# Expert slots: turning the tokens with VectorE and ScalarE instead of TensorE

## The chip, the cores and the metric

One core of one Trainium2 chip. The metric is the device time of one execution in microseconds, the median of three runs. The engines are TensorE (matmuls, PE in the profile; its weight loads are PEld), VectorE (DVE), ScalarE (ACT), GpSimd (POOL) and SyncE (SP, which issues most transfers).

## The reference: what is computed

Three stages over 4608 tokens of 512 values, all in float32:

```python
kv  = einsum('bhsd,bhse->bhde', k, v)           # attention without softmax, 8 batches, 8 heads
x   = rmsnorm(einsum('bhsd,bhde->bhse', q, kv)) * g_norm    # 4608 x 512
h   = x @ w_in                                  # 512 -> 2048
x   = gate(h) @ w_out                           # gate: h above 1, 0 below -1, (h+1)**2/4 between
e   = argmax(normalised x @ normalised expert_emb.T / tau)  # one of 8 experts per token
out = softmax_weight * (relu(x @ w1[e]) @ w2[e])            # 512 -> 1024 -> 512
```

## The kernel before, in words

The attention and the dense block come first (up to about 945 us). Each tile of 128 tokens that leaves the dense block is routed: its rows, 512 values and 16 of bookkeeping (`ROW` is 528), are scattered to the region of their expert in `xs`. Then come the expert **slots**. A slot is one tile of up to 128 tokens that share an expert; there are at most 43 (`NSLOT`), and 41 are run before a branch that asks whether more are wanted. The first four (`FULL`) belong to an expert that is known early, and have code of their own; slots 4 and on read a table, made by VectorE, of which rows, which expert and which half of the weight ring they use.

What a slot does:

- `x_load` (L750) brings the tile `xr[t]` from `xs`, tokens on partitions. `loads_ahead` issues it four slots ahead (`X_AHEAD`); seven buffers (`xr`, `row`) hold tiles.
- The tile is turned, so that the 512 values lie on partitions, in four blocks of 128. Before the change TensorE does it: `tr_x` (L768) issues four transposes by an identity (L771) into a PSUM bank `xp`, right after layer 1 of the slot before; `split_x` (L774) then has ScalarE copy the bank as fp32r, `x[:, 0]` (L778), and VectorE subtract that copy from the bank (helper `sub`, L192), so that `x[:, 1]` holds what the rounding left over.
- Layer 1, `l1` (L842): 24 matmuls of 128x128 by 512 columns. Four blocks by two halves of the 1024 hidden values, each as three products (`PASSES`: high by high, high by low, low by high).
- For slots 4 and on, `turn_h` (L888) turns the 1024 hidden values: VectorE transposes squares of 32x32, 16 instructions of 32 partitions by 256 elements from PSUM (L897). Host code laid out `w1` so that the squares land where layer 2 wants them. `split_h` (L904) makes the two halves of `hT` with ReLU: ScalarE's copy (L912), VectorE's subtraction (L914), twice.
- Layer 2, `l2` (L920): 24 matmuls. `finish` (L927) weighs the rows (ScalarE's `ex`, L932, and `ys`, L938; two small VectorE operations) and GpSimd scatters them to `out` (L941).

TensorE's order is written by `slots`: layer 1 of slot t, the transposes for slot t+1, layer 2 of slot t-1. So the work of VectorE and ScalarE on a slot has most of a slot's time to finish.

The order on the other engines comes from a planner, `Flow`: each piece of work is a generator that yields the engine and an estimated cost ahead of every instruction, `ev` for events and `get` for buffers. The piece that could start first goes next on its engine; among those within 0.05 us, the lower priority number. `turn_h` and `split_h` have 0, `finish` 0.5. Every engine then runs its instructions in the order that the planner wrote.

Weights lie in two rings of two halves, `ra` (layer 1) and `rb` (layer 2). `load_next` (L786) is called once per slot and ring, but moves data only in the first slot of an expert (`cond`), for the expert after it: two transfers of 2 MB each (L807), once the half to be filled is no longer read by TensorE and the loads before it on the same ring have landed.

Of the kernel before, what the change touches and what calls it, by code (L numbers as in the profile page):

```python
# [7 lines left out]
F32 = mybir.dt.float32  # L8
F32R = mybir.dt.float32r
# [3 lines left out]
AF = mybir.ActivationFunctionType  # L13
# [5 lines left out]
P = 128  # L19
# [3 lines left out]
DM = 512  # L23
# [6 lines left out]
ROW = 528  # L30
# [123 lines left out]
def tile_kernel(ctx: ExitStack, tc: tile.TileContext, qT, k, v, g2, w_in, w_out, emb, tau, w1, w2, cst, tri, out):  # L154
    nc = tc.nc
# [6 lines left out]
    NSLOT = TOK // P + NE - 1  # L162
# [4 lines left out]
    FULL = (NBLK - 1) * TB // NE // P  # L167
# [7 lines left out]
    keep = ctx.enter_context(tc.tile_pool(name="keep", bufs=1))  # L175
# [6 lines left out]
    f = Flow()  # L182

    def bank(name, tag, shape=(P, DM), bufs=1):
        return ps.tile(list(shape), F32, name=name, tag=tag, bufs=bufs)
# [5 lines left out]
    def sub(eng, out_, a, hi):  # L191
        eng.tensor_tensor(out=out_, in0=a, in1=hi.bitcast(F32), op=ALU.subtract)  # L192
# [10 lines left out]
    for name, n in {  # L203
        "h": 2, "cl": 2, "g": 2, "xT": 2, "sp": 2, "raw0": 1, "raw1": 1, "raw2": 1, "raw3": 1, "t0": 1, "t1": 1, "t2": 1, "t3": 1, **{f"kv{i}": 1 for i in range(7)}, "qt": 1, "xk": 1, "op": 1, "xp": 1, "kvp": 1,
        "kvd0": 1, "kvd1": 1, "acc0": 1, "acc1": 1, "acc2": 1, "row": NTB, "r": 1, "xr": 4, "hb00": 1, "hb01": 1, "hb10": 1, "hb11": 1,
        "y0": 1, "y1": 1, "xT2": 2, "ht": 2, "hT": 2, "small": 1, "dots": 1,
    }.items():
        f.put(name, n)


    kvd2 = keep.tile([P, 2 * 4 * P], F32, name="kvd2")
    nc.gpsimd.memset(kvd2, 0.0)
    kvd = [kvd2[:, i * 4 * P : (i + 1) * 4 * P].rearrange("p (a c) -> p a c", a=4) for i in range(2)]
    consts_ = {}
# [268 lines left out]
    dots = {}  # L483
# [61 lines left out]
    pools = {}  # L545
# [183 lines left out]
    xr = {}  # L729
    xT2 = {}  # L730
    ht = {}
    hT = {}
# [3 lines left out]
    def reg(eng, ap, hi, lo=0):  # L736
        return eng.value_load(ap, min_val=lo, max_val=hi)
# [30 lines left out]
    def tr_x(t):  # L768
        xp = bank("xp2", "xp", (P, 4, P))
        for c in range(4):  # L770
            nc.tensor.transpose(out=xp[:, c], in_=xr[t][:, c * P : c * P + P], identity=consts_["cs"][:, 0:P])  # L771
        return xp

    def split_x(t, xp):  # L774
        yield "get", "xT2"
        yield "act", 0.48
        x = xT2[t] = pools["x"].tile([P, 2, 4, P], F32R, name="xT2", tag="xT2", bufs=2)
        nc.scalar.activation(out=x[:, 0], in_=xp, func=AF.Copy)  # L778
        yield "dve", 0.6
        sub(nc.vector, x[:, 1], xp, x[:, 0])  # L780
        f.put("xp")
        f.set(("x2", t))

    loads = {"a": [None, None], "b": [None, None]}

    def load_next(t, which):  # L786
# [30 lines left out]
    def product(out, lhsT, t, which, c0, start, stop):  # L817
        ring = ra if which == "a" else rb
        if t < FULL:
            nc.tensor.matmul(out=out, lhsT=lhsT, rhs=ring[:, 0, c0 : c0 + 512], start=start, stop=stop)  # L820
            return
        m = nc.tensor.matmul(  # L822
            out=out, lhsT=lhsT, rhs=ring[:, bass.ds(pars[t], 1), c0 : c0 + 512].rearrange("p a f -> p (a f)"),
            start=start, stop=stop,
        )
        cur, prev = loads[which]
        for d in cur:
            tc.declare_no_dep(_ins(m), _ins(d), reason="the load fills the other half of the ring")
        if prev is not None:
            for q, d in enumerate(prev):  # L830
                if q == c0 // (8192 // NPC):
                    need(m, d, "an earlier load filled this half of the ring")
                else:
                    tc.declare_no_dep(_ins(m), _ins(d), reason="the load fills other columns")
# [3 lines left out]
    def hb(t, hf):  # L838

        return f"hb{0 if t < FULL else t % 2}{hf}"  # L840

    def l1(t):  # L842
        x = xT2[t]
        for hf in range(2):
            yield "get", hb(t, hf)
            for dk in range(4):
                yield "pe", 0.71
                if dk == hf == 0 and t >= FULL:
                    pars[t] = reg(nc.tensor, ord_["sch"][t : t + 1, 3:4], 1)
                if dk == 0:  # L850
                    h = bank("h2", HB[hb(t, hf)], bufs=2 if HB[hb(t, hf)] == "h" else 1)
                for n, (xa, wa) in enumerate(PASSES):
                    product(
                        h, x[:, xa, dk], t, "a", dk * 2048 + wa * 1024 + hf * 512, dk == 0 and n == 0,
                        dk == 3 and n == 2,
                    )
            f.add(relu(t, hf, h) if t < FULL else turn_h(t, hf, h), 0)

    def relu(t, hf, h):
        if hf == 0:  # L860
            yield "get", "ht"
            ht[t] = pools["h"].tile([P, 8, P], F32, name="hr", tag="ht", bufs=2)
        yield "act", 0.6
        nc.scalar.activation(
            out=ht[t].rearrange("p c (q a) -> p q c a", q=4)[:, 2 * hf : 2 * hf + 2],
            in_=h.rearrange("p (q c a) -> p q c a", q=2, c=8), func=AF.Relu,
        )
        f.put(hb(t, hf))
        f.set(("hs", t, hf))
# [18 lines left out]
    def turn_h(t, hf, h):  # L888

        if hf == 0:  # L890
            yield "get", "ht"
            ht[t] = pools["h"].tile([P, 8, P], F32, name="ht", tag="ht", bufs=2)
        for i in range(4):
            for q in range(2):
                yield "dve", 0.36
                r, s = slice(32 * i, 32 * i + 32), slice(64 * hf + 32 * q, 64 * hf + 32 * q + 32)
                nc.vector.transpose(  # L897
                    out=ht[t][s, :, r], in_=h[r, 256 * q : 256 * q + 256].rearrange("p (c a) -> p c a", c=8)
                )
        f.put(f"hb{t % 2}{hf}")  # L900
        if hf == 1:
            f.add(split_h(t), 0)
# [17 lines left out]
    def l2(t, fcs):  # L920
        if fcs[0] == 0:
            yps[t] = bank("y", f"acc{t % 2}")
        for fc in fcs:
            for n, (ga, wa) in enumerate(PASSES):
                product(yps[t], hT[t][:, ga, fc], t, "b", fc * 1024 + wa * 512, fc == 0 and n == 0, fc == 7 and n == 2)
# [240 lines left out]
    def loads_ahead(t):  # L1166
        if FULL <= t < NSLOT:
            yield "ev", "table"
            yield "get", "xr"
            yield "sp", 2.9 if t == FULL else 1.9 if t < FULL + NE - 1 else 0.9  # L1170
            x_load(t)

    def slots(start, end):

        for t in range(start, end + 1):
            if t < end:
                f.add(loads_ahead(t + X_AHEAD), 0)
                f.set(("slot", t))
                yield "ev", ("x2", t)
                if t == 0:  # L1180
                    for q in range(4):
                        yield "ev", ("ring", "a", q)
                yield from l1(t)
                if FULL <= t + 1 < NSLOT:
                    yield "ev", "table"
                    load_next(t + 1, "a")
                f.put("xT2")
                if t + 1 < NSLOT:
                    yield "ev", ("xr", t + 1)
                    yield "get", "xp"  # L1190
                    yield "pe", 0.43
                    f.add(split_x(t + 1, tr_x(t + 1)), 0)
            if t > start:
                yield "get", f"y{(t - 1) % 2}"
                if t == 1:
                    for q in range(4):
                        yield "ev", ("ring", "b", q)
            for n in range(2):
                if t > start:
                    yield "ev", ("hT", t - 1, n)  # L1200
                    yield "pe", 2.81
                    l2(t - 1, range(4 * n, 4 * n + 4))
                if t < min(end, FULL):
                    if n == 0:
                        yield "get", "hT"
                        for hf in range(2):
                            yield "ev", ("hs", t, hf)
                    yield "get", f"hb1{n}"
                    yield "pe", 0.43
                    f.add(split_hp(t, n, tr_h(t, n)), 0)  # L1210
                    if n == 1:
                        f.put("ht")
            if t > start:
                f.put("hT")
                f.add(finish(t - 1), 0.5)
            if FULL <= t < end:
                load_next(t, "b")

    f.add(make_table(), 1)
    f.add(slots(0, SURE), 5)  # L1220
    f.add(second_expert(), 2)
    f.run()
    used = nc.values_load(ord_["sch"][0:1, 5:6], min_val=1, max_val=NSLOT)  # L1223
    with tc.If(used > SURE):
        f.add(slots(SURE, NSLOT), 5)
        f.run()
# [47 lines left out]
```

## Time and profile before

| what | value |
|---|---|
| median of three runs | 1448.8 us (1446.64 to 1449.76) |
| the profiled execution's own time | 1447.99 us |
| its span, first to last instruction | 1446.2 us |
| busy share of TensorE, VectorE, ScalarE, GpSimd | 96%, 77%, 43%, 26% |
| expert slots, first layer 1 to the last instruction | from about 945 us to the end |

The profile is of one execution. Busy time of TensorE is modelled, since its matmuls overlap; when it waited is read better from the list of waits, and how fast it ran from the starts in the timeline. A line of the timeline merges instructions of one kind: start, time to the end of the last, engine, line, operation, tiles, count; behind it in brackets the idle time before it and what ended that. "128x512 f32" is partitions by elements.

### The profile page before, as it was taken

How to read it: one execution, taken by the hardware profiler on the slowest of the kernel's cores; microseconds unless marked ns; L12 is line 12 of the kernel's file. 1: busy time of each engine (PE TensorE's matmuls, PEld its weight loads, DVE VectorE, ACT ScalarE, POOL GpSimd, SP SyncE). 2: the span in 40 equal slices, each digit the busy share in tenths (PEclk: the TensorE clock that was granted, in tenths of full speed). 3: DMA queues.
4: the chain of work that ended last, by engine and by line, in shares of the span. 5: the costliest groups of instructions: out<-in, count | busy, mean ns of one | idle time of the engine just before them, and what ended most of it. 6: DMA issues, size and time to landing. Idle time of an engine off the chain costs nothing. (4 is left out here: it accounts for less than half of the span.)

```text
span 1446.2 us, 24714 instructions
## 1 busy us (share of the span) xinstructions
PE 1391.8 (96%) x7474; PEld 1194.2 (83%) x7474; DVE 1120.5 (77%) x2629; ACT 618.5 (43%) x1259; POOL 377.0 (26%) x347
## 2 busy tenths in 40 slices
PE   6889999999999999999999999999999999999995
PEld 5768889889889888888889999878888888888884
DVE  5888989696969797978778756485887778888883
ACT  4766455545555554555555534332222222222221
POOL 1675233323233332333332332310000010000000
PEclk9999999999999999999999999999999999999998
DMA  9764654555655564545454200583111137774175
GB/s 290 240 223 169 204 193 166 190 196 183 216 191 177 176 232 170 180 167 180 164 181 162 69 31 1 222 334 112 53 46 45 46 136 278 273 288 178 46 298 207
DMA packets 85456, 249.99 MB, mean 173 GB/s; under 512 B 10190, under 2 KB 10446, under 8 KB 80592
## 3 DMA queue, kind: packets, MB, share of 16 engines
q1 hardware_dynamic: 79168, 229.21, 44.9%
q0 software_dynamic: 6160, 19.18, 3.4%
q8 instruction: 68, 1.11, 0.3%
q14 instruction: 60, 0.49, 0.1%
HBM read 423.87 MB, written 90.02 MB: 355 GB/s over the span
## 5 line engine op out<-in xcount | busy, mean ns | idle before, releaser
L1048 PE MATMUL acc<-rb,g 128*128 128x512 f32 x1728 | 448.5, 400 | 9.9 <-POOL rb L192 6.4
L1025 PE MATMUL h<-xT,ra 128*128 128x384 f32 x2304 | 441.3, 338 | 0.6 <-DVE xT L387 0.4
L1025 PEld LDWEIGHTS h<-xT,ra 128*128 128x128 f32 x2304 | 403.3, 188 | 17.6 <-DVE xT L387 0.6
L1048 PEld LDWEIGHTS acc<-rb,g 128*128 128x128 f32 x1728 | 319.8, 189 | 72.1 <-POOL rb L192 8.8
L897 DVE STREAM_TRANSPOSE ht<-h 32x256 f32<-32x256 f32 x592 | 264.1, 446 | 55.1 <-PE h L822 44.2
L192 POOL TENSOR_TENSOR sp<-sp 128x512 fp32r<-128x512 f32 x128 | 182.3, 1429 | 441.3 <-ACT sp L466 421.8
L561 DVE CUSTOM_DVE_ANT_0 tr<-row,en 128x512 bf16<-128x512 f32 x288 | 228.0, 796 | 3.0 <-ACT row L526 0.3
L822 PE MATMUL y<-rb,hT 128*128 x888 | 217.9, 401 | 5.1 <-DMA rb<-ws 5.1
L822 PE MATMUL h<-ra,xT 128*128 x888 | 213.9, 396 | 0.0
L822 PEld LDWEIGHTS y<-rb,hT 128*128 128x128 f32 x888 | 165.2, 189 | 43.3 <-issue 6.0
L822 PEld LDWEIGHTS h<-ra,xT 128*128 128x128 f32 x888 | 167.1, 188 | 40.4
L964 ACT ACTIVATE h<-h,neg 128x384 f32<-128x384 f32 x176 | 97.6, 554 | 214.8 <-DVE cl L957 214.8
L975 DVE TENSOR_TENSOR cl<-h,cl 128x384 f32<-128x384 f32 x176 | 97.4, 554 | 65.7 <-ACT cl L968 65.5
L980 ACT ACTIVATE g<-cl 128x384 fp32r<-128x384 f32 x192 | 100.7, 525 | 110.2 <-DVE cl L975 70.6
L957 DVE TENSOR_SCALAR cl<-h 128x384 f32<-128x384 f32 x192 | 105.8, 551 | 45.9 <-PE h L1025 44.9
L192 DVE TENSOR_TENSOR g<-cl,g 128x384 fp32r<-128x384 f32 x144 | 100.6, 698 | 31.9 <-ACT g L980 30.4
L968 ACT ACTIVATE cl<-cl,half 128x384 f32<-128x384 f32 x192 | 116.6, 607 | 0.0
L912 ACT ACTIVATE hT<-ht 128x512 fp32r<-128x512 f32 x74 | 46.2, 624 | 160.4 <-DVE ht L897 160.4
L941 POOL DMA_INDIRECT out<-ys,xr x24 | 23.4, 974 | 269.0 <-ACT ys L938 241.7
L778 ACT ACTIVATE xT<-xp 128x512 fp32r<-128x512 f32 x42 | 25.1, 598 | 159.3 <-PE xp L771 159.2
L466 ACT ACTIVATE sp<-sp 128x512 fp32r<-128x512 f32 x128 | 79.2, 622 | 12.6 <-DMA sp<-in_w 11.2
L192 POOL TENSOR_TENSOR g<-cl,g 128x384 fp32r<-128x384 f32 x48 | 53.4, 1113 | 88.8 <-ACT g L980 85.9
(156 smaller groups left out, 1079.2 us busy)
## 6 DMA issues: line engine op xcount, KB each, us to landing
ra<-ws SPq DMA_DIRECT2D x78, 2048.0 KB
rb<-ws SPq DMA_DIRECT2D x76, 2048.0 KB
ws<-sp SPq DMA_DIRECT2D x128, 512.0 KB
sp<-in_w SPq DMA_DIRECT2D x128, 256.0 KB
qt<-in_qT SPq DMA_DIRECT2D x33, 256.0 KB
raw<-in_w_in SPq DMA_DIRECT2D x16, 512.0 KB
raw<-in_w_out SPq DMA_DIRECT2D x16, 512.0 KB
kt<-in_k SPq DMA_DIRECT2D x26, 256.0 KB
```

The costliest lines, as they stand in the source:

```text
L192: eng.tensor_tensor(out=out_, in0=a, in1=hi.bitcast(F32), op=ALU.subtract)
L466: nc.scalar.activation(out=sp[:, 0], in_=r, func=AF.Copy)
L561: nc.vector.tensor_tensor_reduce(out=trash("tr", e % 2), in0=rows[blk, t][:, 0:DM], in1=en[:, e], scale=1.0, scalar=0.0, op0=ALU.mult, op1 ...
L822: m = nc.tensor.matmul(out=out, lhsT=lhsT, rhs=ring[:, bass.ds(pars[t], 1), c0 : c0 + 512].rearrange("p a f -> p (a f)"), start=start, sto ...
L897: nc.vector.transpose(out=ht[t][s, :, r], in_=h[r, 256 * q : 256 * q + 256].rearrange("p (c a) -> p c a", c=8))
L957: nc.vector.tensor_scalar(out=cl, in0=h, scalar1=-1.0, scalar2=1.0, op0=ALU.max, op1=ALU.min)
L964: nc.scalar.activation(out=over, in_=h, func=AF.Relu, bias=consts_["neg1"])
L968: nc.scalar.activation(out=cl, in_=cl, func=AF.Square, bias=consts_["half"], scale=0.5)
L975: nc.vector.tensor_tensor(out=cl, in0=over, in1=cl, op=ALU.add)
L980: nc.scalar.activation(out=g[:, 0], in_=cl, func=AF.Copy)
L1025: nc.tensor.matmul(out=h, lhsT=ra[:, wa, o : o + P], rhs=xT[blk][:, xa, dk], start=dk == 0 and n == 0, stop=dk == 3 and n == 2,)
L1048: nc.tensor.matmul(out=accs[t], lhsT=g[:, ga, t * P : t * P + P], rhs=rb[:, wa, df * 512 : df * 512 + 512], start=(df == 0 and n == 0), st ...
```

## The change

For slots 4 and on, TensorE's four transposes and their PSUM bank go. A new piece of work, `turn_x`, starts as layer 1 of the slot before starts. VectorE transposes the 128x512 tile in squares of 32x32, one instruction, into `xt`. This leaves each square turned, but in the quadrant of 32 partitions in which it was read. ScalarE then copies 32 partitions by 4x32 elements sixteen times, from quadrant i of `xt` to quadrant q of `xf`. From `xf`, in SBUF, the two halves of `xT2` are made as before: ScalarE's copy as fp32r, VectorE's subtraction. `xt` lies behind the padding rows in `kvd2`, which grows by 16 columns for it; `xt` and `xf` have one buffer each. Tiles 0 to 3 still go through TensorE.

```diff
--- before.py
+++ after.py
@@ -203,12 +203,12 @@
     for name, n in {
         "h": 2, "cl": 2, "g": 2, "xT": 2, "sp": 2, "raw0": 1, "raw1": 1, "raw2": 1, "raw3": 1, "t0": 1, "t1": 1, "t2": 1, "t3": 1, **{f"kv{i}": 1 for i in range(7)}, "qt": 1, "xk": 1, "op": 1, "xp": 1, "kvp": 1,
         "kvd0": 1, "kvd1": 1, "acc0": 1, "acc1": 1, "acc2": 1, "row": NTB, "r": 1, "xr": 4, "hb00": 1, "hb01": 1, "hb10": 1, "hb11": 1,
-        "y0": 1, "y1": 1, "xT2": 2, "ht": 2, "hT": 2, "small": 1, "dots": 1,
+        "y0": 1, "y1": 1, "xT2": 2, "ht": 2, "xt": 1, "xf": 1, "hT": 2, "small": 1, "dots": 1,
     }.items():
         f.put(name, n)
 
 
-    kvd2 = keep.tile([P, 2 * 4 * P], F32, name="kvd2")
+    kvd2 = keep.tile([P, 2 * 4 * P + ROW - DM], F32, name="kvd2")
     nc.gpsimd.memset(kvd2, 0.0)
     kvd = [kvd2[:, i * 4 * P : (i + 1) * 4 * P].rearrange("p (a c) -> p a c", a=4) for i in range(2)]
     consts_ = {}
@@ -781,6 +781,31 @@
         f.put("xp")
         f.set(("x2", t))
 
+    def turn_x(t):
+
+        yield "ev", ("xr", t)
+        yield "get", "xt"
+        yield "dve", 0.65
+        xt = kvd2[:, ROW : ROW + DM]
+        nc.vector.transpose(out=xt, in_=xr[t][:, 0:DM])
+        xt = xt.rearrange("p (c q b) -> p c q b", c=4, q=4)
+        yield "get", "xf"
+        xf = pools["h"].tile([P, 4, P], F32, name="xf")
+        for i in range(4):
+            for q in range(4):
+                yield "act", 0.29
+                r = slice(32 * i, 32 * i + 32)
+                nc.scalar.activation(out=xf[32 * q : 32 * q + 32, :, r], in_=xt[r, :, q], func=AF.Copy)
+        f.put("xt")
+        yield "get", "xT2"
+        yield "act", 0.6
+        x = xT2[t] = pools["x"].tile([P, 2, 4, P], F32R, name="xT2", tag="xT2", bufs=2)
+        nc.scalar.activation(out=x[:, 0], in_=xf, func=AF.Copy)
+        yield "dve", 0.65
+        sub(nc.vector, x[:, 1], xf, x[:, 0])
+        f.put("xf")
+        f.set(("x2", t))
+
     loads = {"a": [None, None], "b": [None, None]}
 
     def load_next(t, which):
@@ -1180,12 +1205,14 @@
                 if t == 0:
                     for q in range(4):
                         yield "ev", ("ring", "a", q)
+                if FULL <= t + 1 < NSLOT:
+                    f.add(turn_x(t + 1), 1)
                 yield from l1(t)
                 if FULL <= t + 1 < NSLOT:
                     yield "ev", "table"
                     load_next(t + 1, "a")
                 f.put("xT2")
-                if t + 1 < NSLOT:
+                if t + 1 < min(FULL, NSLOT):
                     yield "ev", ("xr", t + 1)
                     yield "get", "xp"
                     yield "pe", 0.43
```

## Rows read from the trace of the kernel before

**Rows 1.** The page: span, and busy time of TensorE.

```profile
span 1446.2 us, 24714 instructions
...
PE 1391.8 (96%) x7474; PEld 1194.2 (83%) x7474; DVE 1120.5 (77%) x2629; ACT 618.5 (43%) x1259; POOL 377.0 (26%) x347
```

**Rows 2.** Waits, 1003 to 1437 us, of TensorE: sum, times, longest.

```profile
PE y L822 <- DMA rb<-ws: 5.1, 2, 4.1
```

**Rows 3.** Timeline of TensorE, one slot: start, us, instructions.

```profile
1248.04 5.78 PE L822 MATMUL h<-ra,xT 128*128 x24
1253.65 0.60 PE L771 MATMUL xp<-cs,row 128*128 128x128 f32 x4
1254.01 5.84 PE L822 MATMUL y<-rb,hT 128*128 x24
1259.69 5.78 PE L822 MATMUL h<-ra,xT 128*128 x24
```

**Rows 4.** Timeline of TensorE, last full slot, behind the `hp` transposes.

```profile
979.10 5.86 PE L820 MATMUL h<-ra,xT 128*128 128x512 f32 x24
984.80 0.60 PE L771 MATMUL xp<-cs,row 128*128 128x128 f32 x4
```

**Rows 5.** Windows, 35 slots: length, busy per engine, clock, DMA share, GB/s.

```profile
1003.36:1411.16 407.80, 407.80 (x1821) 329.59 (x1820) 326.84 (x735) 92.16 (x211) 33.99 (x35) 1.00 0.41 153
```

**Rows 6.** Groups of ScalarE by form: instruction, count, busy and mean ns, idle.

```profile
L778 ACT ACTIVATE xT<-xp 128x512 fp32r<-128x512 f32 x42 | 25.1, 598 | 159.3 <-PE xp L771 159.2
...
L306 ACT ACTIVATE kvd<-kvp 64x256 f32<-64x256 f32 x16 | 6.0, 376 | 6.0 <-PE kvp L293 5.9
```

**Rows 7.** Timeline of ScalarE, a pair of `kvd` copies.

```profile
30.77 0.77 ACT L306 ACTIVATE kvd<-kvp 64x256 f32<-64x256 f32 x2
```

**Rows 8.** Timeline of ScalarE, end of a slot.

```profile
1259.29 0.63 ACT L912 ACTIVATE hT<-ht 128x512 fp32r<-128x512 f32 x1 [4.34 <-DVE ht L897]
1259.83 0.19 ACT L932 ACTIVATE ex<-row 128x8 f32<-128x8 f32 x1
...
1260.02 0.62 ACT L912 ACTIVATE hT<-ht 128x512 fp32r<-128x512 f32 x1
1260.99 0.69 ACT L938 ACTIVATE ys<-y,gt 128x512 f32<-128x512 f32 x1 [0.36 <-issue]
```

**Rows 9.** Timeline of VectorE, one slot.

```profile
1251.04 5.10 DVE L897 STREAM_TRANSPOSE ht<-h 32x256 f32<-32x256 f32 x11 [1.19 <-PE h L822]
1256.17 0.69 DVE L192 TENSOR_TENSOR xT<-xp,xT 128x512 fp32r<-128x512 f32 x1
1256.89 2.31 DVE L897 STREAM_TRANSPOSE ht<-h 32x256 f32<-32x256 f32 x5
1259.96 0.69 DVE L914 SCALAR_TENSOR_TENSOR hT<-ht,hT 128x512 fp32r<-128x512 f32 x1 [0.76 <-ACT hT L912]
...
1260.83 0.67 DVE L914 SCALAR_TENSOR_TENSOR hT<-ht,hT 128x512 fp32r<-128x512 f32 x1
```

**Rows 10.** Groups of VectorE by form, the fastest of 128x512 f32.

```profile
L511 DVE TENSOR_SCALAR en<-en,ess 128x512 f32<-128x512 f32 x8 | 3.7, 500 | 0.0
```

**Rows 11.** Timeline of the DMA queue of SyncE, weight loads of the end.

```profile
1382.02 1.62 SPq L807 DMA_DIRECT2D ra<-ws  x2
...
1395.70 1.62 SPq L807 DMA_DIRECT2D ra<-ws  x2
...
1419.75 1.63 SPq L807 DMA_DIRECT2D rb<-ws  x2
```

**Rows 12.** Waits of that queue, three stretches: 1380, 1390.2 and 1410 us on.

```profile
SPq L807 <- PE h L822: 0.4, 1, 0.4
...
SPq L807 <- DMA ra<-ws: 3.0, 1, 3.0
...
SPq L807 <- DMA rb<-ws: 9.0, 1, 9.0
```

**Rows 13.** Timeline of TensorE, layer 2 of the last slot, first half.

```profile
1427.10 4.58 PE L822 MATMUL y<-rb,hT 128*128 x12 [4.12 <-DMA rb<-ws]
```

## The prediction

> **What bounds the kernel now.** I read the page first: TensorE is busy 96% of a 1446.2 us span [rows 1]. That alone doesn't say that its work is the bound, so the list of waits came next, for the stretch of the expert slots: TensorE waits there for nothing but two weight loads, 5.1 us in all [rows 2], both in the last slot (the longer is [rows 13]). The timeline of one slot shows the loop: 24 matmuls of layer 1, the four transposes `xp`, 24 matmuls of layer 2, then the next slot, 11.65 us in all [rows 3]. [...] So what leaves TensorE's queue here shortens the slot, as long as VectorE stays under the new period.
>
> **What the change takes away.** Layer 1 takes 1253.65 - 1248.04 = 5.61 us, the transposes hold the queue from 1253.65 to 1254.01, 0.36 us, layer 2 takes 5.68 us [rows 3]. The same 24 matmuls therefore take 0.07 us more behind the transposes. Where layer 1 itself stands behind transposes (those of `hp`, ahead of 979.10) it takes 5.70 us instead of 5.61 [rows 4]; I take the surplus as part of their price. New slot: 2 x 5.61 = 11.22 us at most; with the switches between the groups a little less, 11.2. The saving is 0.36 (surplus stays) to 0.45 (it goes); I take 0.44 per slot. Of 42 groups of transposes, counted by the copies that empty them [rows 6], tiles 0 to 3 keep theirs; 38 go, of tiles 4 to 41.
>
> **How many of the 38 count.** At the end the weights bound the slot. The load of `ra` at 1382.02 waited for the end of a layer 1 of TensorE [rows 11, 12]: that of slot 37, since the transposes behind it are the fourth group from the last, those of tile 38. The next load of `ra`, at 1395.70, had waited 3.0 us for the first to land; the `rb` load of the last expert, at 1419.75, had waited 9.0 us for the `rb` load ahead [rows 11, 12]; and layer 2 of the last slot waits 4.12 us for it [rows 13]. From 1382.02 on, the end thus hangs on transfers, and only what TensorE saves before that moves it: the groups of tiles 4 to 37, 34 of them. 34 x 0.44 = 15.0 us; with 0.45 it is 15.3. I take 15.2.
>
> **What it adds on VectorE.** One transpose of 128x512 from SBUF per tile. No such row exists. From below, the fastest 128x512 operation, 0.50 us [rows 10]; from above, two of the 32x256 transposes, 2 x 0.446 = 0.89, at eleven in 5.10 us, 0.46 from start to start [rows 9]. Nearest are the 128x512 operations of the slot, 0.67 to 0.69 [rows 9]; I take 0.70. The subtraction stays and now reads SBUF instead of PSUM: 0.69 as before (0.67 for the one that reads SBUF now).
>
> **What it adds on ScalarE.** Sixteen copies of 32 partitions by 128 elements and the cast (0.62 instead of 0.60). A copy lies between 0.19 us (8 elements) and 0.38 (256 elements) [rows 6, 8]; on the line from 8 elements at 0.19 to 512 at 0.62 it is 0.29. Whether they overlap decides more. In the slot an instruction starts 0.10 us before the one ahead ends (1259.83 against 1259.29 + 0.63) [rows 8]. The two `kvd` copies, which change their partitions from one to the next as the new ones do, take 0.77 for two of 0.38: no overlap, 0.01 more [rows 6, 7]. They are the nearest in kind, so 0.30 to 0.31 a copy, 4.9 us a tile; the ends are 0.19 and 0.39. ScalarE is busy 92/35 = 2.63 us of a slot, so 7.6 of 11.2: room enough.
>
> [...]
>
> **Where it lies.** VectorE's turn through a slot is 11.65 us less its wait for `h` (1.19): 10.46 [rows 9]. In it stands a wait of 0.76 for ScalarE's `hT`, between the last transpose of a slot and the first subtraction. `turn_x` of the next tile is added just as layer 1 starts, which is about then, so its transpose (0.70) falls into or just before that wait, and costs 0 to 0.7. Then three copies (0.9) get ahead of the second `hT` cast on ScalarE, which delays the last subtraction of the slot by some 0.6 once the two small operations are done. I take 0.6 to 0.7 for both: 11.1 to 11.2 us, against TensorE's 11.2. It just fits; the 1.19 us in which VectorE waited for `h` is used up. If it doesn't quite fit, nothing is lost at once: the tile's second half was ready at 1256.86, 2.8 us before layer 1 wanted it at 1259.69 [rows 3, 9], 2.4 us by the new period, and `hT` 4.2 us before layer 2 (1261.50 against 1265.7).
>
> The subtraction is a new risk: VectorE stands still there until ScalarE has done 16 copies and the cast, and the rest of the `h` transposes stand behind it. ScalarE needs 4.9 + 0.63 (second `hT`) + 0.69 (`ys`) + 0.29 (`ex` and its sum) + 0.62 (cast) = 7.1 us after the tile's transpose; VectorE meanwhile has the two subtractions with their waits (2.3) and, if the planner keeps the place after eleven transposes, 5.1: 7.4. It fits by 0.3 us. The planner's costs, 0.29 a copy and 0.65 a transpose, are near mine, so the place should suit. The tile itself is loaded four slots ahead; waiting for it earlier costs nothing.
>
> **Sum.** The profiled execution took 1447.99 us, 0.8 below the median of 1448.8. 1447.99 - 15.2 = 1432.8; on the median's footing 1433.6, which I forecast.
>
> **Rivals.**
> 1. *VectorE becomes the bound.* With the tile's transpose at its upper end (0.89), or not covered, or with copies at 0.32 to 0.35, its turn is 11.3 to 11.7 us. At 11.45 TensorE loses 0.24 a slot once the 2.4 us of lead are gone: 34 x 0.24 - 2.4 = 5.8 us of the gain, so 1439.4; the span of the case is 1436 to 1445. For it: the fit is 0.1 us. Against: two middle values have to be too low together, or one at its end.
> 2. *Slower: the subtraction waits for sixteen dear copies.* At 0.39 a copy ScalarE needs 6.2 + 2.2 = 8.4 us where VectorE has 7.4; VectorE stands 1.0 to 1.1 us in each slot and its turn is 12.2 us, over today's 11.65: 34 x 0.55 - 2.4 = +16, so 1465. It decides from about 0.35 a copy. For it: 0.38 is a row of this kernel. Against: that row has twice the elements.
> 3. *The whole 38 count*, if the last loads start earlier with TensorE and the transfers aren't full: 38 x 0.445 = 16.9, so 1431.9. Against: 3.0 and 9.0 us of waiting for loads [rows 12].
> 4. *It does not do what it says*: TensorE's slot stays 11.65 us since the price of the transposes was a hand-over between layers that stays without them. Then 1448.8. Against: layer 2 to layer 1 has no gap [rows 3].
>
> **How the numbers follow.** Forecast 60%, rival 1 18%, rival 2 10%, rival 3 8%, rival 4 4%. Within 0.2% (2.9 us, about what a measurement of this kernel can tell from no change) is rival 4: 4%; slower is rival 2: 10%; faster the rest: 86%. The likeliest case's own range is 1432 to 1436. The range to report takes in rivals 1 and 3 nearly whole: 1431 to 1444; outside remain rivals 2 and 4 and some of 1, together under 2 in 10.
>
> **What would show it.** Right: `xp` only 4 times; in the slots layer 2 directly behind layer 1 and a period of 11.2 us; both layers' runs of one length, 5.6; VectorE's wait for `h` nearly gone; `rb` still waited for at the end, longer than 4.12 us, and a new wait of about a microsecond in the slot before. Copies of 0.30 with gaps of 0.01; the tile's transpose 0.70. Wrong: waits of TensorE for `xT` in the slots, or of VectorE for ScalarE's cast of `xT` in every slot; a period between 11.3 and 11.7 (rival 1) or above (rival 2); a last load that no longer waits for the load ahead (rival 3).

## The result and the profile after

The changed kernel takes 1432.05 us (median of 4 runs, 1430.68 to 1436.08) against 1448.14 (4 runs, 1446.64 to 1449.76) before. The ratio is 0.9893 with a 95% interval of 0.987 to 0.9916: 16.1 us less, where 15.2 were forecast. The profiled execution took 1432.09 us.

The page of the changed kernel, its head and its part on busy time, beside [rows 1]:

```profile
span 1430.3 us, 24945 instructions
...
PE 1379.6 (96%) x7322; PEld 1185.2 (83%) x7322; DVE 1146.8 (80%) x2667; ACT 806.7 (56%) x1867; POOL 379.1 (27%) x347
```

TensorE's instructions fall by 152, 38 groups of four; ScalarE's rise by 608, 38 times sixteen, and its share from 43% to 56%. As [rows 1] shows, a share of the span names no bound: TensorE's stays at 96%. The list of waits of the slots does (from 1003 us on: who waited for whom, sum, times, longest):

```profile
DVE hT L939 <- ACT hT L937: 29.9, 37, 0.8
...
PE y L847 <- DMA rb<-ws: 5.4, 2, 4.5
...
PEld h L847 <- DVE xT L192: 1.4, 6, 0.3
...
DVE ht L922 <- PE h L847: 0.4, 1, 0.4
```

VectorE no longer waits for TensorE's `h`, except once. It waited 1.19 us in every slot before [rows 9]. TensorE's own waits are the last weights, as in [rows 2], and something new and small: six waits of at most 0.3 us for the tile's second half, `xT`, all in the last six slots. The same list from 930 us on has a seventh wait of this kind. It is in layer 1 of slot 4, which uses the first tile that is turned in the new way, and makes the step to layer 1 of slot 5 11.56 us long:

```profile
PEld h L847 <- DVE xT L192: 1.8, 7, 0.4
...
991.28 6.14 PE L847 MATMUL h<-ra,xT 128*128 x24
...
1002.84 1.33 PE L847 MATMUL h<-ra,xT 128*128 x5
```

Timeline of TensorE, one slot, against [rows 3]:

```profile
1226.96 5.78 PE L847 MATMUL h<-ra,xT 128*128 x24
1232.58 5.76 PE L847 MATMUL y<-rb,hT 128*128 x24
1238.18 0.63 PE L847 MATMUL h<-ra,xT 128*128 x2
```

Layer 2 starts directly behind layer 1 (5.62 us later), and takes 5.60, not 5.68: the surplus behind the transposes went with them. The slot is 11.22 us against 11.65. VectorE and ScalarE in the same slot, against [rows 9] and [rows 8]:

```profile
1225.94 0.69 DVE L192 TENSOR_TENSOR xT<-xf,xT 128x512 fp32r<-128x512 f32 x1
...
1228.55 0.71 DVE L790 STREAM_TRANSPOSE kvd<-row 128x512 f32<-128x512 f32 x1
1229.22 0.69 DVE L939 SCALAR_TENSOR_TENSOR hT<-ht,hT 128x512 fp32r<-128x512 f32 x1
...
1230.98 0.69 DVE L939 SCALAR_TENSOR_TENSOR hT<-ht,hT 128x512 fp32r<-128x512 f32 x1 [0.81 <-ACT hT L937]
1231.70 5.48 DVE L922 STREAM_TRANSPOSE ht<-h 32x256 f32<-32x256 f32 x12
1237.21 0.69 DVE L192 TENSOR_TENSOR xT<-xf,xT 128x512 fp32r<-128x512 f32 x1
1237.93 1.85 DVE L922 STREAM_TRANSPOSE ht<-h 32x256 f32<-32x256 f32 x4
1239.81 0.71 DVE L790 STREAM_TRANSPOSE kvd<-row 128x512 f32<-128x512 f32 x1
```

```profile
1228.55 0.63 ACT L937 ACTIVATE hT<-ht 128x512 fp32r<-128x512 f32 x1 [3.46 <-DVE ht L922]
...
1229.35 0.95 ACT L798 ACTIVATE xf<-kvd 32x128 f32<-32x128 f32 x3
1230.32 0.63 ACT L937 ACTIVATE hT<-ht 128x512 fp32r<-128x512 f32 x1
...
1231.55 4.14 ACT L798 ACTIVATE xf<-kvd 32x128 f32<-32x128 f32 x13
1235.73 0.63 ACT L803 ACTIVATE xT<-xf 128x512 fp32r<-128x512 f32 x1
```

VectorE's turn, from one transpose of a tile (L790) to the next, is 1239.81 - 1228.55 = 11.26 us and has no wait for TensorE in it. That is longer than TensorE's 11.21. So VectorE falls behind by 0.06 us a slot, and each slot the tile is ready that much later: here at 1237.90, 0.28 us before layer 1 starts; one slot earlier at 1226.63, 0.33 us before. Some 20 slots earlier, for tile 6, this lead was 1.5 us (1012.57, layer 1 at 1014.04). Layer 1 uses the second half only from its third matmul on, so the lead is used up when the tile comes some 0.4 us behind the start. That is about five slots before the end; from there on TensorE goes at VectorE's pace, 11.27. The windows view over 35 slots, against [rows 5]:

```profile
1002.84:1395.26 392.42, 392.42 (x1681) 315.77 (x1680) 351.66 (x766) 265.02 (x770) 34.04 (x35) 1.00 0.42 158
```

392.42 us for 35 slots, 11.21 each; VectorE busy in 351.66 and ScalarE in 265.02.

The weight loads of the end, in the timeline of SyncE's queue, and the wait of the last one and TensorE's for it, against [rows 11 to 13]:

```profile
1367.34 1.62 SPq L832 DMA_DIRECT2D ra<-ws  x2
...
1380.37 1.63 SPq L832 DMA_DIRECT2D ra<-ws  x2
...
1404.05 1.64 SPq L832 DMA_DIRECT2D rb<-ws  x2
```

```profile
SPq L832 <- DMA rb<-ws: 9.0, 1, 9.0
```

```profile
1411.56 4.34 PE L847 MATMUL y<-rb,hT 128*128 x12 [4.49 <-DMA rb<-ws]
```

The chain of loads is as it was, 1 us shorter: 36.71 us from the `ra` load to the last `rb` load, 37.73 before.

### The profile page after: what moved, and what is told of

It reads as the page before. It is cut to its first block, busy times and chain, and to the rows that moved or that the text cites. A ratio compares the mean times of both kernels' runs of the same rounds, so it can differ in the third digit from the quotient of the medians.

```text
span 1430.3 us, 24945 instructions
## 1 busy us (share of the span) xinstructions
PE 1379.6 (96%) x7322; PEld 1185.2 (83%) x7322; DVE 1146.8 (80%) x2667; ACT 806.7 (56%) x1867; POOL 379.1 (27%) x347
## 5 line engine op out<-in xcount | busy, mean ns | idle before, releaser
L1050 PE MATMUL h<-xT,ra 128*128 128x384 f32 x2304 | 446.5, 340 | 0.3 <-DVE xT L387 0.3
L1050 PEld LDWEIGHTS h<-xT,ra 128*128 128x128 f32 x2304 | 408.3, 188 | 17.0 <-DVE xT L387 0.5
L847 PE MATMUL y<-rb,hT 128*128 x888 | 214.6, 397 | 5.5 <-DMA rb<-ws 5.4
L798 ACT ACTIVATE xf<-kvd 32x128 f32<-32x128 f32 x608 | 187.2, 308 | 7.5 <-DVE kvd L790 0.4
```

The costliest lines, as they stand in the source:

```text
L798: nc.scalar.activation(out=xf[32 * q : 32 * q + 32, :, r], in_=xt[r, :, q], func=AF.Copy)
L847: m = nc.tensor.matmul(out=out, lhsT=lhsT, rhs=ring[:, bass.ds(pars[t], 1), c0 : c0 + 512].rearrange("p a f -> p (a f)"), start=start, sto ...
L1050: nc.tensor.matmul(out=h, lhsT=ra[:, wa, o : o + P], rhs=xT[blk][:, xa, dk], start=dk == 0 and n == 0, stop=dk == 3 and n == 2,)
```

## The experiments

Runs of one kernel scatter by 3 us and more. In the profiles most of the scatter lies ahead of the slots, in code that the edits don't touch: the first layer 1 of a slot started anywhere from 942.6 to 950.5 us (but for one, named below). What the edits do is read from the traces, in two stretches: **head**, from the first layer 1 to the `ra` load behind layer 1 of slot 37; **tail**, from that load to the end of the span. Heads of kernels that are alike up to slot 37 agree within 0.4 us: 422.1 and 422.2 for the changed kernel, 436.9 and 436.5 for the one before and the one with new turns from tile 38 on. The ratios are to the kernel before on the same chip.

| kernel | head, us | tail, us | time, us | ratio, 95% interval |
|---|---|---|---|---|
| before | 436.9 | 64.2 | 1448.1 | 1 |
| changed | 422.1 | 63.0 | 1432.1 | 0.9893 (0.987 to 0.9916) |
| changed, second set | 422.2 | 62.3 | 1433.2 | 0.991 (0.9884 to 0.9935) |
| no turn | 421.7 | 63.7 | 1437.3 | 0.9931 (0.9918 to 0.9944) |
| new turn for tiles 4 to 37 | 422.1 | 62.7 | 1436.8 | 0.993 (0.9917 to 0.9943) |
| new turn for tiles 38 to 41 | 436.5 | 64.6 | 1450.4 | 1.0019 (1.0006 to 1.0032) |
| subtraction on GpSimd | 422.7 | 64.1 | 1436.0 | 0.9927 (0.9914 to 0.994) |
| VectorE's transpose twice | 445.8 | 64.1 | 1457.8 | 1.0068 (1.0042 to 1.0093) |
| 8 copies more, unplanned | 482.8 | 67.5 | 1501.5 | 1.0377 (1.0355 to 1.0398) |
| 8 copies more, planned | 426.9 | 63.5 | 1440.5 | 0.9961 (0.9945 to 0.9977) |
| copies in their quadrant | 421.7 | 64.2 | 1438.1 | one run |
| copies planned dearer | 422.1 | 63.7 | 1435.4 | 0.9915 (0.9887 to 0.9944) |
| all tiles | 426.6 | 64.6 | 1438.3 | 0.9918 (0.9891 to 0.9945) |
| all tiles, planned dearer | 427.0 | 63.8 | 1442.0 | 0.9942 (0.9916 to 0.9969) |

**The changed kernel again**, beside the second set.

> The changed kernel once more, beside the others of this set. From its first layer 1 of a slot to its end the changed kernel took 485.1 us, the kernel before 501.1; the part ahead of the slots, which both have in common, began the slots anywhere from 942.6 to 949.4 us in six profiles. Expected: 484.5 to 485.5 for the slots, and a total of 1430 to 1437 that follows the part ahead.

Head 422.2, tail 62.3: 484.5 us for the slots, as expected.

**Which tiles count.** Two halves of the change. For tiles 4 to 37, and in the other kernel with `38 <= t + 1 < NSLOT`:

```diff
-                if FULL <= t + 1 < NSLOT:
+                if FULL <= t + 1 < 38:
                     f.add(turn_x(t + 1), 1)
...
-                if t + 1 < min(FULL, NSLOT):
+                if t + 1 < NSLOT and not FULL <= t + 1 < 38:
```

> The new turn for tiles 4 to 37, TensorE's transposes for tiles 38 to 41. Theory A (after layer 1 of slot 37 the end hangs on weight transfers): the same time as the changed kernel, within 0.7 us. Rival B (all 38 groups count): 4 x 0.44 = 1.8 us slower than it. In the trace A expects the wait for the last rb load to be about 1.3 us shorter than with all 38 turned, at the same end.

> The counterpart: the new turn for tiles 38 to 41 alone. Theory A (the end hangs on weight transfers from layer 1 of slot 37 on): the time of before, 1448, within 0.7 us, and the wait for the last rb load grows by the 1 to 1.8 us that TensorE gains. Rival B (all groups count): 1.8 us faster than before, 1446.4.

Tiles 4 to 37 alone have the whole gain: slots of 484.8 us against 485.1 and 484.5. Tiles 38 to 41 alone have none: 501.1 against 501.1 before. Both medians, 1436.8 and 1450.4, lie above what was expected, by 4.8 and 2.4 us; the slots don't account for that, see the end of the next section. TensorE in the last two slots, new turn for tiles 38 to 41:

```profile
1413.02 5.78 PE L847 MATMUL h<-ra,xT 128*128 x24
1418.64 2.97 PE L847 MATMUL y<-rb,hT 128*128 x12
1422.99 3.04 PE L847 MATMUL y<-rb,hT 128*128 x12 [1.38 <-DMA rb<-ws]
1430.37 5.46 PE L847 MATMUL y<-rb,hT 128*128 x12 [4.34 <-DMA rb<-ws]
```

and with the new turn for tiles 4 to 37:

```profile
1406.61 5.82 PE L847 MATMUL y<-rb,hT 128*128 x24
1415.01 4.59 PE L847 MATMUL y<-rb,hT 128*128 x12 [2.57 <-DMA rb<-ws]
```

What TensorE gains on the last four tiles it waits for in layer 2 of slot 39 (1.38 us, a wait that the kernel before doesn't have) and of slot 40; where the last four tiles keep TensorE's transposes, the wait for the last load is 2.57 us instead of 4.49, and the end stays. For the slots theory A holds. The twelve matmuls behind the wait of 4.34 us take 5.46 us, the twelve at 1418.64 only 2.97: from 1429.8 to 1436.5 the granted clock was 0.50, and TensorE had stood still for 4.34 us just before.

**No turn at all.** The tile as loaded goes straight to the cast and the subtraction.

```diff
-        xt = kvd2[:, ROW : ROW + DM]
-        nc.vector.transpose(out=xt, in_=xr[t][:, 0:DM])
...
-        xf = pools["h"].tile([P, 4, P], F32, name="xf")
-        ... (the sixteen copies)
+        xf = xr[t][:, 0:DM].rearrange("p (c a) -> p c a", c=4)
```

> Left out: the turn itself (VectorE's transpose and ScalarE's sixteen copies); the two halves of the tile are made from the tile as it was loaded, so the output is not the reference's. Theory A (TensorE sets the slot nearly to the end, VectorE's added work costs almost nothing): the period of a slot is 11.20 to 11.21 us in every slot, and the time is 0.3 to 1 us under the changed kernel's, 1431 to 1432. Rival B (VectorE's turn of 11.27 us has been the bound through all 34 slots since the first): 34 x 0.06 = 2 us or more under it, below 1430. Rival C (sixteen copies disturb TensorE or the transfers in some other way): below 1428.

From slot 5 on every slot takes 11.19 to 11.22 us, to the last. The head is 421.7 against 422.1: all that VectorE and ScalarE now do for the turn costs the slots 0.4 us. Most of that comes once, at tile 4. From layer 1 of slot 4 to that of slot 5 it is 11.27 us here and 11.56 in the changed kernel:

```profile
992.56 5.86 PE L838 MATMUL h<-ra,xT 128*128 x24
...
1003.83 5.78 PE L838 MATMUL h<-ra,xT 128*128 x24
```

VectorE's pace of 11.27 us adds 0.1 us up to the end of the head (0.2 in the second set), and 0.2 to 0.3 by the start of slot 40, where the loads set the end. The total, 1437.3, was above the expected one; the slots (485.3 us) don't account for that, see the end of the next section.

**The subtraction on GpSimd.**

```diff
-        yield "dve", 0.65
-        sub(nc.vector, x[:, 1], xf, x[:, 0])
+        yield "pool", 1.4
+        sub(nc.gpsimd, x[:, 1], xf, x[:, 0])
```

> The changed kernel with the tile's subtraction on GpSimd, which is idle in the slots, instead of VectorE. Theory A (VectorE's turn through a slot, 11.27 us against TensorE's 11.21, eats 0.06 us of lead a slot and reaches TensorE only in the last six slots): VectorE's turn falls to about 10.6 us, it waits for h again in each slot (0.5 us or more), no slot of TensorE is longer than 11.21, and the time is 0.3 to 0.6 us less than the changed kernel's, 1431.5: hardly to be told from it. Rival B (GpSimd's 1.4 us instruction slows VectorE's or makes the tile late): TensorE waits for the tile in every slot, 1435 or more.

VectorE waits for `h` again, in the waits of the slots:

```profile
DVE ht L922 <- PE h L847: 33.5, 35, 1.0
```

and no later slot exceeds 11.22 us. But tile 4 comes later still: TensorE waits 0.62 us for it, slot 4 takes 12.18 us instead of 11.56, and the head is 422.7, no better. The median of 1436.0 lies where rival B put it, but the wait in every slot that rival B names isn't there. That VectorE's pace took its toll late is borne out; what there is to win is under the scatter of the times.

**The subtraction as a risk: its place in VectorE's order.** Three edits of the changed kernel. VectorE's transpose twice:

```diff
         nc.vector.transpose(out=xt, in_=xr[t][:, 0:DM])
+        nc.vector.transpose(out=xt, in_=xr[t][:, 0:DM])
```

and eight copies more, into a scratch tile `xe`, behind the sixteenth; the planned kernel has `yield "act", 0.29` ahead of each:

```diff
+        for n in range(8):
+            nc.scalar.activation(out=xe[32 * (n % 4) : 32 * (n % 4) + 32],
+                in_=xt[32 * (n // 4) : 32 * (n // 4) + 32, :, n % 4], func=AF.Copy)
```

> VectorE's transpose of the tile is issued twice (0.72 us more per tile, the same result), with no cost given to the planner, so the order stays. Theory A (VectorE's turn through a slot is an order of instructions with one wait for ScalarE in it, 11.27 us long, so what is added there adds to it): turn 11.99 us; the lead of 2.4 us is gone after four slots, TensorE then waits for the tile in every slot, 11.99 instead of 11.21: 34 x 0.78 - 2.4 = 24 us more than the changed kernel in the slots, about 509, slower than before. Rival B (VectorE is busy only 10.05 of 11.21 us, so 0.72 still fits): within 2 us of the changed kernel, 485 to 487.

> ScalarE makes eight more copies of 32x128 per tile, into a scratch tile, right behind the sixteenth, with no cost given to the planner, so VectorE's order stays. 8 x 0.318 = 2.54 us. Theory A (second rival of the prediction: VectorE stands at the tile's subtraction until ScalarE is through, with 0.8 us to spare now): VectorE's turn is 11.27 + 2.54 - 0.8 = 13.0 us, TensorE's slot too: 34 x 1.8 - 2.4 = 59 us more in the slots, about 544. Rival B (throughput decides: ScalarE would be busy 7.6 + 2.5 = 10.1 us of 11.21): within 2 us of the changed kernel, 485 to 487.

> The same eight copies, but the planner is told of them (0.29 us each), so it writes VectorE's subtraction further back, behind more of the transposes of h. Theory A (only the place in the order made the wait): VectorE's turn stays near 11.3 us, the tile is ready about 2.3 us later than now, right when layer 1 wants it: slots of 11.2 to 11.5 us, 485 to 495 us for the slots, far under the unplanned one. Rival B (ScalarE's 24 copies themselves are too long for a slot, whatever the order): near the unplanned one, 520 or more.

The slots took 509.9 us (509 expected), 550.3 (544) and 490.4 (485 to 495). With the transpose twice, TensorE's slot is 12.02 us from slot 9 on, with a wait for the tile in the middle of layer 1:

```profile
1229.21 0.63 PE L848 MATMUL h<-ra,xT 128*128 x2
1230.39 5.42 PE L848 MATMUL h<-ra,xT 128*128 x22 [0.56 <-DVE xT L192]
1235.65 5.74 PE L848 MATMUL y<-rb,hT 128*128 x24
1241.23 0.63 PE L848 MATMUL h<-ra,xT 128*128 x2
```

With the eight unplanned copies VectorE stands at the subtraction, in every slot of 13.03 us; planned, it stands there no longer, and waits for `h`:

```profile
1226.83 0.69 DVE L192 TENSOR_TENSOR xT<-xf,xT 128x512 fp32r<-128x512 f32 x1 [1.79 <-ACT xT L806]
...
1232.60 5.48 DVE L925 STREAM_TRANSPOSE ht<-h 32x256 f32<-32x256 f32 x12
1239.87 0.69 DVE L192 TENSOR_TENSOR xT<-xf,xT 128x512 fp32r<-128x512 f32 x1 [1.80 <-ACT xT L806]
```

```profile
1231.92 0.69 DVE L192 TENSOR_TENSOR xT<-xf,xT 128x512 fp32r<-128x512 f32 x1
1232.59 0.69 DVE L943 SCALAR_TENSOR_TENSOR hT<-ht,hT 128x512 fp32r<-128x512 f32 x1
...
1235.68 7.41 DVE L926 STREAM_TRANSPOSE ht<-h 32x256 f32<-32x256 f32 x16 [0.95 <-PE h L851]
```

The same work on ScalarE, 24 copies a tile, costs 1.8 us in every slot or nothing, by where VectorE's subtraction stands: after twelve transposes of `h` it waits; after all sixteen it falls into the wait that VectorE has for ScalarE's `hT` anyway (0.81 us in the changed kernel, none here). That the planned kernel still has a head of 426.9 is tile 4, late once by 3.2 us, and the clock behind that wait: from 996.0 to 999.3 us the granted clock was 0.50, and layer 1 of slot 4 took 7.4 us, 6.0 in the changed kernel.

**The order alone.**

```diff
-                yield "act", 0.29
+                yield "act", 0.29 if t < 7 else 0.44
```

> The changed kernel with nothing else than the planner's cost of a copy raised from 0.29 to 0.44 us for tiles 7 and on, so that it writes the tile's subtraction behind nearly all transposes of h, where VectorE otherwise waits for ScalarE. Theory A (the order makes VectorE's turn): turn 10.25 us instead of 11.27, a wait for h of 0.95 us in each slot as in the run with eight more planned copies, no slot over 11.21, 484.6 us for the slots against 484.5 to 485.1 of the changed kernel. Rival B (the order helped there for another reason): turn 11.2 to 11.3 and the lead shrinks as before.

```profile
1225.27 0.69 DVE L192 TENSOR_TENSOR xT<-xf,xT 128x512 fp32r<-128x512 f32 x1
1225.94 0.69 DVE L939 SCALAR_TENSOR_TENSOR hT<-ht,hT 128x512 fp32r<-128x512 f32 x1
...
1226.81 0.69 DVE L790 STREAM_TRANSPOSE kvd<-row 128x512 f32<-128x512 f32 x1
...
1229.03 7.42 DVE L922 STREAM_TRANSPOSE ht<-h 32x256 f32<-32x256 f32 x16 [0.96 <-PE h L847]
1236.48 0.69 DVE L192 TENSOR_TENSOR xT<-xf,xT 128x512 fp32r<-128x512 f32 x1
```

Theory A holds for VectorE: the subtraction stands behind the sixteenth transpose, VectorE waits 0.96 us for `h`, no slot from slot 8 on is longer than 11.22. The head is that of the changed kernel, 422.1: the order gives VectorE 1 us a slot, and there is nothing for TensorE to gain by it. So VectorE's pace isn't most of what the changed kernel's head has above the 421.7 without a turn; slot 4 is 11.56 us here too.

**All tiles.** The new turn for tiles 1 to 3 too, alone and with the dearer plan.

```diff
-                if FULL <= t + 1 < NSLOT:
+                if t + 1 < NSLOT:
                     f.add(turn_x(t + 1), 1)
...
-                if t + 1 < min(FULL, NSLOT):
+                if False:
```

> The new turn for tiles 1 to 3 as well; only tile 0 keeps TensorE. Theory A (TensorE bounds the first slots too): 3 x 0.44 = 1.3 us less, about 483.5 us for the slots. Rival B (in the first slots ScalarE has four more passes and VectorE makes the table, so the tiles come late and TensorE waits): 486 us or more.

> Both together: the new turn for tiles 1 to 3, and the copies of tiles 7 and on planned at 0.44 us. Expected if both theories hold: 483.2 us for the slots, the least of all, with no slot from the sixth on over 11.21; if the first slots wait, 486 or more with the later slots still at 11.21.

Rival B: slots of 491.2 and 490.8 us. TensorE in the first two slots (in this profile the slots began at 954.9):

```profile
954.91 5.79 PE L845 MATMUL h<-ra,xT 128*128 128x512 f32 x24
963.63 1.97 PE L901 MATMUL hp<-cs,hr 128*128 128x128 f32 x8 [2.93 <-ACT hr L889]
966.94 7.67 PE L845 MATMUL h<-ra,xT 128*128 128x512 f32 x24 [1.34 <-ACT xT L803]
```

With TensorE's transposes of tile 1 gone, those of `hp` come at once behind layer 1 of slot 0 and wait 2.93 us for ScalarE, which has the copies of tile 1 in its queue, and layer 1 of slot 1 waits 1.34 for that tile. It then takes 7.67 us instead of 5.79: the granted clock was 0.50 from 963.6 to 967.2, just behind the first of these waits, and 0.77 over this layer. The first slots hang on ScalarE, not on TensorE.

**The price of a copy.**

```diff
-nc.scalar.activation(out=xf[32 * q : 32 * q + 32, :, r], in_=xt[r, :, q], func=AF.Copy)
+nc.scalar.activation(out=xf[r, :, 32 * q : 32 * q + 32], in_=xt[r, :, q], func=AF.Copy)
```

> Left out: the move between quadrants. Each of the sixteen copies writes to the 32 partitions from which it reads, so twelve of sixteen have the partitions of the copy before them, and the output is not the reference's. In the changed kernel a copy takes 0.308 us and the next starts 0.318 after it. Theory A (a change of partitions from one ScalarE instruction to the next ends their overlap, as in the kvd pair): twelve copies start about 0.21 apart and four 0.318, 3.8 us instead of 5.1. Rival B (short copies from SBUF never overlap): all 0.318, 5.1 us.

```profile
1233.14 0.71 ACT L798 ACTIVATE xf<-kvd 32x128 f32<-32x128 f32 x3
...
1234.86 3.04 ACT L798 ACTIVATE xf<-kvd 32x128 f32<-32x128 f32 x13
```

Thirteen copies take 3.04 us where they took 4.14. Of their starts, those with the partitions of the copy ahead lie 0.20 to 0.22 us apart, those that change them 0.30 to 0.31. In the changed kernel all lie 0.32 apart and each takes 0.308. Theory A. With these shorter copies slot 4 takes 11.28 us and the head is 421.7, so the wait for tile 4 in the changed kernel is a wait for ScalarE.

## Why the prediction was right, point by point

- **The price of the transposes**: 0.44 a slot forecast; 11.65 - 11.21 measured, and the surplus of 0.07 to 0.09 in the group behind went with them. With the no-turn kernel the saving per tile up to the first load is (436.9 - 421.7)/34 = 0.447.
- **34 of 38 count**: shown by the two halves. In the head 14.7 to 14.8 us were saved (436.9 to 422.1 and 422.2); 15.2 were forecast, and the no-turn kernel has the 15.2. Of the missing 0.4 to 0.5 about 0.3 is tile 4, late once behind ScalarE's copies, for which the forecast had no term; VectorE's pace has 0.1 to 0.2 of it.
- **VectorE's turn**: the term that was sized too low, 11.1 to 11.2 forecast, 11.27 measured. The transpose of the tile, 0.71, took the place of the wait of 0.76 ahead of the first subtraction of `hT`, as the forecast allowed at best. But the three copies ahead of the second `hT` cast made a new wait of 0.81 ahead of the second subtraction, where some 0.6 was forecast. What kept it from mattering was the lead. It was not the 2.4 us of the forecast but 1.5 at tile 6, and 0.4 more until layer 1 uses the second half: at 0.06 a slot that lasts some 30 slots, nearly to the end. Rival 1 is true as a mechanism, at the foot of its range (11.3), and cost 0.1 to 0.2 us ahead of the last loads; by an estimate from these numbers a kernel with twice as many slots would go at 11.27 in its second half.
- **ScalarE's chain**: 0.305 a copy forecast, 0.318 measured. The planner set the subtraction after twelve transposes, not eleven, which gave 0.8 us to spare, where 0.3 were forecast. Rival 2 is shown as a mechanism by the unplanned copies. By an estimate from these 0.8 us it begins at 0.05 more a copy (0.37); no run tried that.
- **The overlap of the copies**: none was forecast, after the `kvd` pair of [rows 7], and in the changed kernel there is none: 0.308 us a copy, the next 0.318 after it. An overlap was found among these copies where they keep their partitions, with the copies in their quadrant, and only there (0.295 us each, starts 0.20 to 0.22 apart).
- **The tail**: forecast unchanged. It came out 1.2 us shorter in the changed kernel's profile and 1.9 in the second, but lay between 62.7 and 64.6 us in all others except the unplanned copies, without order by what they change. It is where the 16.1 us exceed the 14.7, so what the result has beyond the forecast isn't a gain of the mechanism that was forecast; the second set has 14.9. The new wait of about a microsecond in the slot before the last, a sign that the prediction named, is missing in the changed kernel's profile, whose last `rb` load comes 1 us sooner in the tail; it is there with the new turn for tiles 38 to 41 (1.38 us). Why the same loads take 1 to 2 us less in some executions stays open.
- **What stays open**: by the medians the part ahead of the slots took some 2 to 5 us longer in most of the edited kernels than in the one before (for tiles 38 to 41, whose slots are equal: 2.6 us, ratio above 1 by its interval). One profile a kernel can't tell chance from an effect of the moved buffers, and no run was made for it. Part of it goes with the clock: by and large the slower runs of a kernel have the lower mean granted clock (no turn: 1433.7 us at 0.992, 1438.9 at 0.987), and the medians of the no-turn kernel and of the kernel before in its set are 0.990 and 0.992. Why the clock was lower stays open.

No kernel here is measurably better than the changed one.

## What to carry to other kernels

Where one engine has a full queue, a piece moved off it is worth its slot in that queue, here 0.36 us and 0.09 of aftermath, but only until the point from which transfers set the end; count the repetitions up to there. The engines that take the piece over need more than idle time: add up their turn in order, with the waits inside it, and compare it to the new period; if it is a little longer, the lead of the buffers divided by the excess gives the number of rounds that are free. Look at the first rounds by themselves: here the one wait at the first new tile cost more than the excess of all the rounds behind it up to the last loads. An instruction that waits for a long chain on another engine belongs where its engine waits anyway: here, with 24 copies a tile, the slots took 490.4 us so and 550.3 otherwise.

## What the runs showed of the hardware that was not expected

In these kernels a ScalarE copy of 32x128 that read and wrote the partitions of the one ahead started 0.20 to 0.22 us after it; if it changed those that it writes, alone or with those that it reads, 0.30 to 0.32. So the change of partitions cost 0.1 us, a third of such a copy.
